# Pooled attention and two feed-forward layers: the SBUF tiles laid out from multiples of 2048 bytes

## The chip, the cores and the metric

The kernel runs on one core of a Trainium2 chip. The metric is device time in microseconds (us), taken as the median of the runs. The engines are TensorE (PE, with its weight loads shown apart as PEld), VectorE (DVE), ScalarE (ACT), GpSimd (POOL) and SyncE (SP, which here only issues DMAs). SBUF, the memory that the engines read and write, has 128 partitions; a place in it is a byte address within a partition, the same in all 128.

## The reference

Two batches of 12,288 tokens with 128 channels. Keys and values are one pooled and projected map of 768 positions; attention is followed by two feed-forward layers, both 128 to 2048 to 128.

```python
kv_pool = kv.reshape(B, H//4, 4, W//4, 4, C).mean(axis=(2, 4))
k = v = kv_pool.reshape(B, -1, C) @ w_sr            # 768 x 128 a batch
s = scale * (q @ k.T)
a = softmax(s)
x = (a @ v).reshape(B*S, D)                         # 24576 x 128
h = x @ w_in;   x = (h * sigmoid(1.702 * h)) @ w_out
h = relu(x @ w2_in);   out = (h * h) @ w2_out
```

Everything is float32, and the kernel keeps nearly that precision with three products of rounded halves, as told below.

## The kernel before

**Tiling.** Everything is kept transposed, channels on the partitions. The tokens come in 48 blocks of 512 (24 a batch). For each block the kernel does the attention and then the two layers. A layer has 16 slices of 128 hidden units: for each, a product into `h_ps` (weights stationary, `x` moving), an activation on ACT into `g_sb`, a split on DVE and ACT into a high and a low half (`ghl`), and a product into `y_ps` (weights stationary, `ghl` moving).

**Three products for one.** A float32 operand is held as two tiles in the fp32r format, high and low (`mm3`, lines 252 to 256): high by high (line 254), high by low (255) and low by high (256). So each product is a trio of matmuls, each with its own load of 128x128 weights and a moving operand of 512 columns (2048 bytes of a partition), or 384 (1536 bytes) for the scores. The first operand of `mm3` is stationary, the second moves. Who reads what:

- `h_ps`: stationary the weights `w1ih`, `w1il` or `W` (second layer), moving `x` (`x1` in the first layer, `x2` in the second);
- `y_ps`: stationary `w1oh`, `w1ol` or `W`, moving `ghl`;
- `s_ps` (scores): stationary `qq`, moving the keys, `kv0` for batch 0 and `KV` for batch 1;
- `av_ps` (attention times values): stationary the values, in `kv0` for batch 0 and in `KV` for batch 1, moving `ahl`.

The trace writes `kv` for the tile `kv0`; the batch-1 tile appears as `KV`. Blocks 0 and 1 do attention with plain float32 operands, and the first two layer passes do the second product so (line 687).

**Order.** The program has no loops on the chip. Every operation is put on record with a cost and a due time (`Plan.op`), `Plan.order` then simulates the engines with these costs and the number of buffers of each ring (`RINGS`, line 259), and the instructions are emitted in that order. TensorE gets the work of several blocks interleaved; `y_ps` of a slice comes `LAG` = 7 slices after its `h_ps`. A tile's address plays no part in this order.

**Where tiles lie.** A pool (`tc.tile_pool`) is a stretch of SBUF; pools follow one another in the order in which they are opened, and inside a pool tiles follow one another in the order of their first use, each padded to 32 bytes. The pool `cp` holds tiles that live through the kernel (line 281 on), `sp` the rings. The first 16,512 bytes of a partition are taken ahead of `cp` (16 KiB of scratch for DMA descriptors, four small constants). From the tile sizes the start addresses are, as remainders:

| tile (in order) | bytes of a partition | start, mod 2048 | start, mod 128 |
|---|---|---|---|
| `ident`, `wsr`, `pooled`, `kf`, `vf` | 512, 512, 3072, 3072, 3072 | 128, 640, 1152, 128, 1152 | 0 |
| `kv0` (keys and values of batch 0) | 12288 | 128 | 0 |
| `minus`; `w1ih`, `w1il`, `w1oh`, `w1ol` | 512; 8192 each | 128; 640 | 0 |
| `qraw` (2), `ghl` (4), second layer's weights (4), `ahl` (2), `y_sb` (2) | 2048, 8192, 8192, 8192, 2048 | 640 | 0 |
| `st` (3) | 48, padded to 64 | 640, 704, 768 | 0, 64, 0 |
| `p_sb`/`pT_sb` (2), `KV` (batch 1), `qq`, `x1` (2), `x2`, `g_sb` (2), `kvraw` (2) | 12288, 12288, 4096, 4096, 4096, 4096, 2048 | 832 | 64 |

The three `st` tiles take 192 bytes, so all that follows them is shifted by 64 against a grid of 128 bytes. Inside a tile the steps are multiples of 512 bytes (weight slices) or 1536 (halves of the keys), so the remainder mod 128 holds for every operand read from it.

Of the kernel before, what the change touches and what calls it, by code (L numbers as in the profile page):

```python
# [10 lines left out]
F32 = mybir.dt.float32  # L11
F32R = mybir.dt.float32r
# [189 lines left out]
def kernel(  # L202
# [20 lines left out]
    P = 128  # L223
    C, NTOK = qT.shape
    B, _, NK, R = kvT.shape
    DFF = w1i.shape[1]
    TB = 512
    NB = NTOK // TB
    NBB = NB // B
    KT = NK // P  # L230
# [10 lines left out]

    cp = ctx.enter_context(tc.tile_pool(name="cp", bufs=1))
    sp = ctx.enter_context(tc.tile_pool(name="sp", bufs=1))
    pp = ctx.enter_context(tc.tile_pool(name="pp", bufs=1, space=bass.MemoryType.PSUM))
    dp = ctx.enter_context(tc.tile_pool(name="dp", bufs=2, space=bass.MemoryType.DRAM))
    c = COST
# [5 lines left out]
    def mm3(out, a, b, start, stop):  # L252
# [9 lines left out]
        pp=(2, [P, QT * NK], F32, sp), aa=(2, [P, 2, 2 * TB], F32R, sp),  # L262
        q=(2, [P, TB], F32, sp), qq=(1, [P, 2, TB], F32R, sp),
        xx=(2, [P, 2, TB], F32R, sp), x2=(1, [P, 2, TB], F32R, sp),
        yo=(2, [P, TB], F32, sp), st=(3, [P, 12], F32, sp), kv=(2, [P, TB], F32, sp), b1=(1, [P, 4, NK], F32R, sp),
        **{f"w{nm}{x}": (1, [P, 2, 2 * TB], F32R, sp) for nm in ("2i", "2o") for x in "hl"},
    )
    plan = Plan({tag: r[0] for tag, r in RINGS.items()})
# [9 lines left out]
        return T[key]  # L278


    ident = cp.tile([P, P], F32, name="ident")
    wsr = cp.tile([P, C], F32, name="wsr")
    pooled = cp.tile([P, NK], F32, name="pooled")
    kf = cp.tile([P, NK], F32, name="kf")
    vf = cp.tile([P, KT, C], F32, name="vf")
    T["KV", 0] = cp.tile([P, 4, NK], F32R, name="kv0")
    minus = cp.tile([P, P], F32R, name="minus")
    for nm in ("1i", "1o"):
        for x in "hl":
            T["W", nm, x] = cp.tile([P, DFF], F32R, name=f"w{nm}{x}")  # L290
# [528 lines left out]
```

## Time and profile before

| | |
|---|---|
| median of 3 runs | 2607.78 us (2607.28 to 2608.26) |
| profiled execution | 2606.7 us, its span 2604.9 us |
| granted TensorE clock, mean | 0.998 of 2.4 GHz |
| PE busy | 2572.7 us (99%), 11260 matmuls |
| PEld busy | 2098.4 us (81%) |
| DVE busy | 2195.5 us (84%) |
| ACT busy | 1853.7 us (71%) |
| POOL busy | 91.7 us (4%) |

The profiled execution has its own time, and it is taken up to the end of the run; the span goes from its first instruction to its last. Matmuls overlap: the trace gives one an end that is modelled, some 0.39 us after its start for 512 columns, while the next begins after about 0.23 us. What a matmul costs the engine when it is never idle is therefore read from the distance of starts in the timeline; the durations are of use for comparing groups with one another. Starts are shown to 0.01 us, so over a run of n matmuls the mean distance is good to about 10 ns / n.

### The profile page before, as it was taken

The page shows a single profiled execution, that of the slowest core. Times are in us where ns is not written, and L with a number is a line of the kernel's source. Part 1 is how long each engine was busy: PE and PEld are TensorE (multiplying, and loading weights), DVE is VectorE, ACT ScalarE, POOL GpSimd, SP SyncE. Part 2 cuts the span into 40 slices and gives each one's busy share as a digit, 9 for nine tenths or more (in the row PEclk, how much of TensorE's full clock was granted, in tenths as well). Part 3 has the DMA queues.
Part 4 walks back from the last instruction along what each step waited for, and adds up shares of the span by engine and source line. Part 5 has one row for each costly group of instructions (what it writes and reads, how often), then busy time and mean ns, then how long its engine had stood idle before and what let it go on. Part 6 is the DMA issues. An engine that isn't in the chain of part 4 may idle for free.

```text
span 2604.9 us, 29500 instructions
## 1 busy us (share of the span) xinstructions
PE 2572.7 (99%) x11260; PEld 2098.4 (81%) x11260; DVE 2195.5 (84%) x2762; ACT 1853.7 (71%) x2117; POOL 91.7 (4%) x98
## 2 busy tenths in 40 slices
PE   6999999999999999999999999999999999999999
PEld 3678888888888888888888888888888888888887
DVE  7898888888888888888888888888888888888876
ACT  4777767776777677776777677767777677767766
POOL 0000000000000000000000000000000000000000
PEclk9999999999999999999999999999999999999999
DMA  4422332223222422223222322232223222232110
GB/s 175 126 61 61 103 84 61 65 89 93 65 61 73 107 68 61 65 86 84 57 57 81 89 57 57 65 101 62 57 57 95 75 57 57 81 89 57 53 53 13
DMA packets 57790, 192.81 MB, mean 74 GB/s; under 512 B 6064, under 2 KB 10288, under 8 KB 51760
## 3 DMA queue, kind: packets, MB, share of 16 engines
q1 hardware_dynamic: 50736, 178.34, 24.5%
q10 hardware_dynamic: 6912, 12.59, 1.5%
q8 instruction: 88, 1.44, 0.2%
q14 instruction: 54, 0.44, 0.1%
HBM read 105.97 MB, written 84.93 MB: 73 GB/s over the span
## 4 chain that ended last, share of the span: by engine, by line
PE 98%; DVE 1%; DMA 1%; ACT 0%; issue 0%; SPq 0%
PE h_ps L255 14%; PE h_ps L254 14%; PE h_ps L256 14%; PE y_ps L255 13%; PE y_ps L256 13%; PE y_ps L254 13%; PE s_ps L256 2%; PE av_ps L254 2%; PE av_ps L255 2%; PE s_ps L255 2%; PE s_ps L254 2%; PE av_ps L256 2%; PE y_ps L687 1%; DMA kvraw<-in_kvT_dram 1%; PE av_ps L610 0%; PE s_ps L498 0%
## 5 line engine op out<-in xcount | busy, mean ns | idle before, releaser
L678 DVE TENSOR_TENSOR ghl<-g_sb,ghl 128x1024 fp32r<-128x1024 f32 x752 | 917.3, 1225 | 74.6 <-ACT ghl L675 53.6
L664 ACT ACTIVATE g_sb<-h_ps 128x1024 f32<-128x1024 f32 x368 | 378.1, 1028 | 393.8 <-PE h_ps L256 278.1
L677 DVE CAST ghl<-g_sb 128x1024 fp32r<-128x1024 f32 x612 | 460.3, 752 | 202.3 <-ACT g_sb L664 153.9
L667 ACT ACTIVATE g_sb<-h_ps 128x1024 f32<-128x1024 f32 x384 | 394.3, 1027 | 129.5 <-PE h_ps L256 118.8
L670 ACT ACTIVATE g_sb<-g_sb 128x1024 f32<-128x1024 f32 x384 | 407.2, 1060 | 6.5
L254 PE MATMUL h_ps<-x,w1ih 128*128 128x512 f32 x768 | 308.5, 402 | 0.2 <-ACT ghl L664 0.2
L254 PE MATMUL h_ps<-x,W 128*128 128x512 f32 x768 | 306.8, 400 | 0.0
L255 PE MATMUL y_ps<-ghl,W 128*128 128x512 f32 x768 | 303.3, 395 | 1.5 <-DVE st L540 1.2
L255 PE MATMUL h_ps<-x,W 128*128 128x512 f32 x768 | 304.2, 396 | 0.0
L255 PE MATMUL h_ps<-x,w1ih 128*128 128x512 f32 x768 | 303.9, 396 | 0.0
L256 PE MATMUL h_ps<-x,W 128*128 128x512 f32 x768 | 303.1, 395 | 0.0
L256 PE MATMUL h_ps<-x,w1il 128*128 128x512 f32 x768 | 302.7, 394 | 0.0
L256 PE MATMUL y_ps<-ghl,W 128*128 128x512 f32 x768 | 301.1, 392 | 0.0
L254 PE MATMUL y_ps<-ghl,W 128*128 128x512 f32 x768 | 300.6, 391 | 0.3 <-DVE ghl L677 0.3
L255 PE MATMUL y_ps<-ghl,w1oh 128*128 128x512 f32 x736 | 289.5, 393 | 0.0
L256 PE MATMUL y_ps<-ghl,w1ol 128*128 128x512 f32 x736 | 289.1, 393 | 0.0
L254 PE MATMUL y_ps<-ghl,w1oh 128*128 128x512 f32 x736 | 287.1, 390 | 0.0
L603 DVE TENSOR_TENSOR ahl<-pT_sb,ahl 128x1024 fp32r<-128x1024 f32 x138 | 164.7, 1221 | 36.4 <-ACT ahl L602 36.4
L511 DVE TENSOR_REDUCE st<-s_ps 128x1 f32<-128x768 f32 x192 | 182.8, 952 | 11.8 <-PE s_ps L256 3.2
L569 DVE STREAM_TRANSPOSE t_sb<-p_sb 128x768 f32<-128x768 f32 x184 | 179.4, 975 | 3.3
L515 ACT ACTIVATE p_sb<-s_ps,st 128x768 f32<-128x768 f32 x192 | 172.9, 901 | 3.3 <-DVE st L511 2.7
L255 PEld LDWEIGHTS y_ps<-ghl,W 128*128 128x128 f32 x768 | 144.3, 188 | 36.9 <-DVE ghl L678 2.9
(104 smaller groups left out, 3797.1 us busy)
## 6 DMA issues: line engine op xcount, KB each, us to landing
way<-t_sb SPq DMA_DIRECT2D x46, 1536.0 KB, 5.1
pT_sb<-way SPq DMA_DIRECT2D x184, 384.0 KB, 7.0
qraw<-in_qT_dram SPq DMA_DIRECT2D x48, 256.0 KB, 9.2
out_dram<-y_sb ACTq DMA_DIRECT2D x48, 256.0 KB, 4.7
kvraw<-in_kvT_dram SPq DMA_DIRECT2D x12, 512.0 KB, 8.8
kvraw<-in_kvT_dram SPq DMA_DIRECT2D x24, 256.0 KB, 7.8
wraw<-in_w1i_dram SPq DMA_DIRECT2D x4, 512.0 KB, 10.3
wraw<-in_w1o_dram SPq DMA_DIRECT2D x4, 512.0 KB, 10.4
```

What stands on the lines that cost most here:

```text
L254: nc.tensor.matmul(out, ah, bh, start=start, stop=False)
L255: nc.tensor.matmul(out, ah, bl, start=False, stop=False)
L256: nc.tensor.matmul(out, al, bh, start=False, stop=stop)
L511: lambda both=both, col=col: nc.vector.tensor_reduce(out=col(0), in_=both(), axis=AX.XY, op=ALU.max, negate=True),
L515: lambda both=both, col=col, p=p: nc.scalar.activation(p().rearrange("p (k a q i) -> p a q k i", k=KT, a=2, q=2) if f32 else p().rearrange ...
L569: plan.op("DVE", c["trans"], at, lambda t=t, p=p: nc.vector.transpose(get(tt)[:, :, t, :], p().rearrange("p (b j) -> p b j", j=32)), reads ...
L603: plan.op("DVE", c["sub1k"], at, lambda ah=ah, al=al, src=src: nc.vector.tensor_sub(four(al()), src(), four(v32(ah()))), reads=[*parts, h] ...
L664: "ACT", c["ev2"], at, lambda G=G, flat=flat: nc.scalar.activation(G(), flat(), AF.Gelu_apprx_sigmoid),
L667: plan.op("ACT", c["ev2"], at, lambda G=G, flat=flat: nc.scalar.activation(G(), flat(), AF.Relu), reads=[(h, 0), (h, 1)], writes=[g])
L670: plan.op("ACT", c["act1k"], at + 0.3, lambda G=G: nc.scalar.activation(G(), G(), AF.Square), writes=[g])
L677: plan.op("DVE", c["cast1k"], at + 0.5, lambda G=G, GH=GH: nc.vector.tensor_copy(GH(), G()), reads=[g], writes=[gh])
L678: plan.op("DVE", c["sub1k"], at + 0.7, lambda G=G, GH=GH, GL=GL: nc.vector.tensor_sub(GL(), G(), v32(GH())), reads=[g, gh], writes=[gl])
```

## The change

A third pool, `ep`, is opened behind `sp`. `pooled`, `kf`, `vf` and the three `st` tiles move there. A tile named `gap` of 384 bytes, which nothing reads or writes, goes ahead of `ident`, and `minus` goes ahead of `kv0`.

```diff
+    ep = ctx.enter_context(tc.tile_pool(name="ep", bufs=1))
...
-        ... st=(3, [P, 12], F32, sp), ...
+        ... st=(3, [P, 12], F32, ep), ...
...
+    cp.tile([P, 96], F32, name="gap")
     ident = cp.tile([P, P], F32, name="ident")
     wsr = cp.tile([P, C], F32, name="wsr")
-    pooled = cp.tile([P, NK], F32, name="pooled")
-    kf = cp.tile([P, NK], F32, name="kf")
-    vf = cp.tile([P, KT, C], F32, name="vf")
+    minus = cp.tile([P, P], F32R, name="minus")
     T["KV", 0] = cp.tile([P, 4, NK], F32R, name="kv0")
-    minus = cp.tile([P, P], F32R, name="minus")
+    pooled = ep.tile([P, NK], F32, name="pooled")
+    kf = ep.tile([P, NK], F32, name="kf")
+    vf = ep.tile([P, KT, C], F32, name="vf")
```

By the sizes, `kv0` now starts at 16,512 + 384 + 3 x 512 = 18,432 = 9 x 2048, and as every later tile of `cp` and `sp` has a multiple of 2048 bytes, all of them start at a multiple of 2048: the weights of both layers, `qraw`, `ghl`, `ahl`, `KV`, `qq`, `x1`, `x2`, and with them `g_sb`, `p_sb`, `pT_sb` and `y_sb`. `pooled` and `vf` start at multiples of 2048 behind them, `kf` and the three `st` tiles follow there. The number of instructions, their order, and what each computes stay as they are.

## Rows read from the trace of the kernel before

**Rows 1.** The page: span, TensorE's busy time, the chain that ended last by engine.
```profile
span 2604.9 us, 29500 instructions
PE 2572.7 (99%) x11260; PEld 2098.4 (81%) x11260; DVE 2195.5 (84%) x2762; ACT 1853.7 (71%) x2117; POOL 91.7 (4%) x98
...
PE 98%; DVE 1%; DMA 1%; ACT 0%; issue 0%; SPq 0%
```

**Rows 2.** Busy us (and instructions) by engine in two stretches, granted clock, DMA share.
```profile
0.00:65.00 65.00, 39.72 (x120) 22.62 (x120) 50.86 (x84) 27.77 (x48) 2.57 (x8) 0.92 0.47 175
...
400.00:600.00 200.00, 200.00 (x888) 165.18 (x887) 172.49 (x215) 142.28 (x160) 8.00 (x8) 1.00 0.30 81
```

**Rows 3.** Waits: who waited for whom, us in total, times, longest.
```profile
PE k_ps L404 <- DMA kvraw<-in_kvT_dram: 13.8, 1, 13.8
...
ACT g_sb L664 <- PE h_ps L256: 278.1, 238, 2.8
```

**Rows 4.** Groups of TensorE by line and tile: count, busy us, mean ns.
```profile
L256 PE MATMUL h_ps<-x,W 128*128 128x512 f32 x768 | 303.1, 395 | 0.0
...
L256 PE MATMUL y_ps<-ghl,W 128*128 128x512 f32 x768 | 301.1, 392 | 0.0
...
L256 PE MATMUL y_ps<-ghl,w1ol 128*128 128x512 f32 x736 | 289.1, 393 | 0.0
...
L256 PE MATMUL s_ps<-KV,qq 128*128 128x384 f32 x192 | 65.1, 339 | 0.0
...
L256 PE MATMUL s_ps<-kv,qq 128*128 128x384 f32 x176 | 59.3, 337 | 0.0
...
L256 PE MATMUL av_ps<-ahl,KV 128*128 128x512 f32 x144 | 56.8, 395 | 0.0
...
L256 PE MATMUL av_ps<-ahl,kv 128*128 128x512 f32 x132 | 51.5, 390 | 0.0
```

**Rows 5.** Timeline of TensorE, a trio of each layer product: start us, us.
```profile
1000.54 0.40 PE L254 MATMUL h_ps<-x,w1ih 128*128 128x512 f32 x1
...
1001.24 0.39 PE L254 MATMUL y_ps<-ghl,W 128*128 128x512 f32 x1
...
1001.93 0.40 PE L254 MATMUL h_ps<-x,w1ih 128*128 128x512 f32 x1
```

**Rows 6.** Timeline of TensorE where batch 0 multiplies by its values.
```profile
973.12 0.39 PE L254 MATMUL av_ps<-ahl,kv 128*128 128x512 f32 x1
...
974.50 0.39 PE L254 MATMUL av_ps<-ahl,kv 128*128 128x512 f32 x1
...
975.85 0.34 PE L254 MATMUL s_ps<-kv,qq 128*128 128x384 f32 x1
...
977.59 0.40 PE L254 MATMUL av_ps<-ahl,kv 128*128 128x512 f32 x1
...
978.98 0.40 PE L254 MATMUL h_ps<-x,W 128*128 128x512 f32 x1
```

**Rows 7.** The same in batch 1.
```profile
1979.51 0.40 PE L254 MATMUL av_ps<-ahl,KV 128*128 128x512 f32 x1
...
1982.31 0.34 PE L254 MATMUL s_ps<-KV,qq 128*128 128x384 f32 x1
...
1983.36 0.39 PE L254 MATMUL y_ps<-ghl,w1oh 128*128 128x512 f32 x1
...
1984.04 0.39 PE L254 MATMUL av_ps<-ahl,KV 128*128 128x512 f32 x1
...
1985.41 0.40 PE L254 MATMUL h_ps<-x,W 128*128 128x512 f32 x1
```

More of the change, by code (lines that the diff above doesn't have):

```diff
@@ L264 @@
         xx=(2, [P, 2, TB], F32R, sp), x2=(1, [P, 2, TB], F32R, sp),
-        yo=(2, [P, TB], F32, sp), st=(3, [P, 12], F32, sp), kv=(2, [P, TB], F32, sp), b1=(1, [P, 4, NK], F32R, sp),
+        yo=(2, [P, TB], F32, sp), st=(3, [P, 12], F32, ep), kv=(2, [P, TB], F32, sp), b1=(1, [P, 4, NK], F32R, sp),
         **{f"w{nm}{x}": (1, [P, 2, 2 * TB], F32R, sp) for nm in ("2i", "2o") for x in "hl"},
```

## The prediction

> **What bounds the kernel now.** I read four views, in this order. First the page's busy times and the chain that ended last: TensorE is busy for 2572.7 of the 2604.9 us of the span and carries 98% of the chain [rows 1]. So the time is what TensorE's instructions cost, laid end to end. Then the stretches: in the first 65 us TensorE works for 39.72 us only, at a granted clock of 0.92; in a steady stretch of 200 us it is busy for all 200.00 us at 1.00, while DVE is busy for 172.49 and ACT for 142.28 us [rows 2]. Third the waits: the longest in which TensorE waits for anybody is 13.8 us, once, for the first keys; in the steady part the waits run the other way, ACT waiting for `h_ps` 238 times, 278.1 us in total [rows 3]. No engine holds TensorE up, and none would until it became some 14% faster (200.00 to 172.49).
>
> So the one question is what a matmul costs, and whether its operands' places have a part in it. That is the fourth view, the timeline: the distance from one start to the next where TensorE is never idle. The granted clock of 1.00 is the level of 2.4 GHz, at which 512 columns take 512 / 2.4 = 213.3 ns. What is seen is more:
>
> - a trio of `h_ps`: 1001.24 - 1000.54 = 0.70 us, 233.3 ns a matmul [rows 5];
> - a trio of `y_ps`: 1001.93 - 1001.24 = 0.69 us, 230.0 ns [rows 5]. Three starts shown to 0.01 us would not separate the two by themselves, but the mean durations of the whole run stand apart the same way, 395 ns for `h_ps` against 392 and 393 for `y_ps` [rows 4];
> - `av_ps` in batch 0: 12 matmuls in 975.85 - 973.12 = 2.73 us and 6 in 978.98 - 977.59 = 1.39 us, so 4.12 us / 18 = 228.9 ns [rows 6];
> - `av_ps` in batch 1: 2.80 us for 12 and 1.37 us for 6, so 4.17 / 18 = 231.7 ns [rows 7].
>
> **The experiment that the kernel before contains.** The last two lines are the same instruction, the same moving tile `ahl`, the same neighbours; what differs is where the stationary values lie: `kv0` starts at a multiple of 128 bytes, `KV` 64 past one (the layout table). The price is 2.8 ns a matmul, and the durations of all of them say so too, 395 against 390 ns [rows 4]. The scores repeat it with the moving operand: 339 ns on `KV`, 337 on `kv0` [rows 4]. And `x1` and `x2`, which move in `h_ps`, lie 64 past such a multiple, while `ghl`, which moves in `y_ps`, lies on one. All three pairs point one way: an operand that starts 64 bytes off a grid of 128 costs TensorE 2 to 3 ns a matmul, whether it is stationary or moving. After the change no operand is off that grid.
>
> **The change part by part.**
>
> The shift of `x1` and `x2` onto the grid: 4608 matmuls of `h_ps` (six groups like the row of 768). The nearest row for a matmul with both operands on the grid is `av_ps` of batch 0 at 228.9 ns, because there, unlike in `y_ps`, no neighbour inside the run is off it. From 233.3 this is 4.4 ns, 20.3 us. The bounds: to the level of `y_ps`, 230.0 ns (15.2 us), and to the lowest level of any trio, 226.7 ns (30.4 us), which is the `y_ps` between 1983.36 and 1984.04: 0.68 us / 3 [rows 7]; the last six of batch 0's first run are as low, 975.85 - 974.50 = 1.35 us / 6 = 225.0 ns, good to 2 ns [rows 6].
>
> `y_ps`, 4512 matmuls (three groups of 768, three of 736): both operands are on the grid of 128 already. They change in what the trace can't show: they now start at multiples of 2048 instead of 128 past a multiple of 512, and their neighbours `h_ps` move onto the grid. I take the level of `av_ps` of batch 0 here too, 1.1 ns, 5.0 us; bounds 0 and, at 226.7 ns, 14.9 us. Below nothing see the second rival.
>
> `KV` of batch 1: 432 matmuls of `av_ps` (three groups of 144) by 2.8 ns, 1.2 us (at 226.7 ns 2.2 us, and 0.9 us for the 396 of batch 0). 576 of `s_ps` (three of 192) by 2 ns, 1.2 us. `qq`, stationary in all 1104 matmuls of `s_ps`, goes onto the grid too: between nothing and the 2.8 ns of `av_ps`, half of it taken, 1.5 us (ends 0 and 3.1).
>
> `pooled`, `kf`, `vf`, `minus`, `ident` and `wsr` are read in the first blocks only, where TensorE waits for keys anyway [rows 2, 3]: nothing. `st`, a few columns for DVE and ACT, nothing. `gap` is never touched. `g_sb`, `p_sb`, `pT_sb` and `y_sb` move for DVE, ACT and the DMAs; should these become slower or faster by some per cent, the cover is the 27.5 us in 200 that DVE is not busy [rows 2]. No wait, DMA or instruction is added or moved.
>
> The sum: 20.3 + 5.0 + 1.2 + 1.2 + 1.5 = 29.2 us. The profiled execution took 2606.7 us, 1.1 below the median of 2607.8; the forecast for the median is 2607.8 - 29.2 = 2578.6 us.
>
> **The rivals.**
>
> Only the grid of 128 counts, and each matmul's level is its own. Then `h_ps` falls to 230.0 ns, `KV` to the level of `kv0`, and the rest stays: 15.2 + 1.2 + 1.2 = 17.6 us, 2590.2 us. For it: `y_ps` is at 230.0 with both operands on the grid. Against it: the same `y_ps` at 226.7 ns in another neighbourhood [rows 7].
>
> The other side: multiples of 2048 are no better than 64 past the grid, and 128 past a multiple of 512 was the good place (all the cheaper rows lie there, and none at a multiple of 256). Then `h_ps` and `KV` stay, and what was cheap rises to their level: `y_ps` to 233.3 ns (3.3 x 4512 = 14.9 us), `av_ps` of batch 0 by 2.8 ns x 396 = 1.1 us, its scores by 2 x 528 = 1.1 us, in all 17.1 us: 2624.9 us. It decides as soon as `y_ps` rises by more than `h_ps` falls. Against it: nothing in the rows says that a rounder address is worse.
>
> Everything on the grid goes to the lowest level, 226.7 ns: 30.4 + 14.9 + 2.2 + 0.9 + 1.2 + 3.1 = 52.7 us, 2555.1 us. For it: that level exists with just such operands [rows 6, 7]. Against it: only in short runs.
>
> All that is over the columns' time is address cost and goes: 213.3 ns, so 20.0 x 4608 + 16.7 x 4512 + 18.4 x 432 + 15.6 x 396 ns = 181.6 us, 2426 us. Against it: no trio is below 226 ns by more than its rounding. The Trainium skill, "TensorE: Matmul & The Clock Gate", section "Back-to-back issue gap", gives N / 2.4 + 2.5 ns for a warm matmul; by that estimate this case would end 9948 x 2.5 ns = 25 us later than with 213.3 ns, and no run of this case shows such a gap.
>
> The layout counts for nothing, and the differences come from the product and its neighbours: 2607.8 us. For it: a `y_ps` trio takes 0.69 us at one place and 0.68 at another, with operands at the same remainders [rows 5, 7]. Against it: rows 6 and 7, equal but for the place. The Trainium skill, "SBUF — State Buffer", sections "Specifications (TRN2)" and "Who interferes with whom", speaks for this rival: its lines are of 16 bytes, all tiles start at whole ones before and after, and TensorE is said never to wait on anyone. By that rule the change is worth 0 us; the trace differs, with 231.7 against 228.9 ns.
>
> **How the numbers follow.** The forecast (2566 to 2584) has 0.36, the grid of 128 alone (2584 to 2602) 0.26, the lowest level (2548 to 2566) 0.14, all address cost gone 0.05, no effect 0.11, slower 0.08. No change means within 0.2% (5.2 us), about what a measurement of this kernel can tell. So faster 0.36 + 0.26 + 0.14 + 0.05 = 0.81, same 0.11, slower 0.08. The range takes in the first three, 0.76, and, drawn to 2604, the edge of no effect: 2548 to 2604.
>
> **What would show it.** In the timeline after, a trio of `h_ps` takes as long as one of `y_ps`, 0.68 to 0.69 us, and 18 `av_ps` of batch 1 as long as 18 of batch 0. The groups' mean durations show no gap between `KV` and `kv`. A steady 200 us holds some 10 matmuls more than 888. TensorE keeps 98% of the chain and DVE's share of the span rises to 85%. I am wrong if `h_ps` keeps 0.70 us with `x` at its new place (the product sets it), if `y_ps` rises (the good place was lost), or if TensorE's idle time grows in the steady part (another engine pays).

## The result, and the profile after

The changed kernel takes 2569.39 us (median of 4 runs, 2568.68 to 2570.12) against 2608.02 us before: a ratio of 0.9852 (95% interval 0.9835 to 0.9869), 38.6 us less. That is 9 us faster than the forecast of 2578.6 us and inside the range (2548 to 2604).

The page of the changed kernel, lines as in [rows 1]:

```profile
span 2566.9 us, 29500 instructions
PE 2534.8 (99%) x11260; PEld 2100.4 (82%) x11260; DVE 2191.0 (85%) x2762; ACT 1852.8 (72%) x2117; POOL 94.5 (4%) x98
...
PE 98%; DVE 1%; DMA 1%; ACT 1%; issue 0%; SPq 0%
```

The span is 38.0 us shorter and TensorE's busy time 37.9 us; the other engines work as long as before. So the whole gain lies in what TensorE's instructions cost. The steady stretch of 200 us (columns as in [rows 2]) says the same:

```profile
400.00:600.00 200.00, 200.00 (x900) 167.75 (x899) 173.56 (x216) 144.68 (x164) 8.19 (x8) 1.00 0.29 81
```

900 matmuls instead of 888, at the same granted clock of 1.00, and TensorE still never idle. ACT goes on waiting for `h_ps`, no less than before [rows 3]:

```profile
ACT g_sb L667 <- PE h_ps L257: 295.7, 227, 2.8
```

The groups of TensorE, as in [rows 4]. In this program the three products of `mm3` stand one line further down, at 255 to 257 (257 is what 256 was), and ACT's line 664 at 667; in the experiments that open a fourth pool `mm3` stands at 256 to 258.

```profile
L257 PE MATMUL h_ps<-x,W 128*128 128x512 f32 x768 | 300.1, 391 | 0.0
L257 PE MATMUL y_ps<-ghl,W 128*128 128x512 f32 x768 | 299.5, 390 | 0.0
...
L257 PE MATMUL y_ps<-ghl,w1ol 128*128 128x512 f32 x736 | 287.8, 391 | 0.0
L257 PE MATMUL s_ps<-KV,qq 128*128 128x384 f32 x192 | 65.5, 341 | 0.0
L257 PE MATMUL s_ps<-kv,qq 128*128 128x384 f32 x176 | 60.0, 341 | 0.0
L257 PE MATMUL av_ps<-ahl,KV 128*128 128x512 f32 x144 | 56.3, 391 | 0.0
L257 PE MATMUL av_ps<-ahl,kv 128*128 128x512 f32 x132 | 51.7, 391 | 0.0
```

These groups of 512 columns (the third product of each trio) now stand at 390 to 391 ns, where the same groups stood between 390 and 395: the difference between `h_ps` and `y_ps` is gone, and the one between `KV` and `kv` too. The scores went the other way, from 337 and 339 to 341 ns.

The timeline of TensorE after, starts first: a trio of `h_ps` and one of `y_ps` [rows 5], the values and scores of batch 0 [rows 6] and of batch 1 [rows 7]:

```profile
961.66 0.39 PE L255 MATMUL av_ps<-ahl,kv 128*128 128x512 f32 x1
...
964.38 0.33 PE L255 MATMUL s_ps<-kv,qq 128*128 128x384 f32 x1
...
965.45 0.39 PE L255 MATMUL y_ps<-ghl,w1oh 128*128 128x512 f32 x1
...
966.15 0.39 PE L255 MATMUL av_ps<-ahl,kv 128*128 128x512 f32 x1
...
967.53 0.39 PE L255 MATMUL h_ps<-x,W 128*128 128x512 f32 x1
...
988.78 0.39 PE L255 MATMUL h_ps<-x,w1ih 128*128 128x512 f32 x1
...
989.46 0.39 PE L255 MATMUL y_ps<-ghl,W 128*128 128x512 f32 x1
...
990.14 0.39 PE L255 MATMUL h_ps<-x,w1ih 128*128 128x512 f32 x1
...
1952.19 0.39 PE L255 MATMUL av_ps<-ahl,KV 128*128 128x512 f32 x1
...
1954.91 0.33 PE L255 MATMUL s_ps<-KV,qq 128*128 128x384 f32 x1
```

Both layer trios take 0.68 us, 226.7 ns a matmul, and 12 matmuls with values take 2.72 us in either batch, 226.7 ns as well (before 2.73 and 2.80 us). That is the level which the prediction called the lowest. Six scores take 965.45 - 964.38 = 1.07 us, and the `y_ps` behind them 0.70 us. Before, these are 1.05 us, from 975.85 [rows 6] to the start of the `y_ps` behind them, and 0.69 us:

```profile
976.90 0.40 PE L254 MATMUL y_ps<-ghl,w1oh 128*128 128x512 f32 x1
...
977.59 0.40 PE L254 MATMUL av_ps<-ahl,kv 128*128 128x512 f32 x1
```

Where the 38 us are, by the mean distance from a matmul's start to the next (worked out from the starts in the two traces; distances of 0.3 us and more, 38 in each trace and nearly all in the first 165 us, are left out): `h_ps` 233.2 to 227.4 ns, 5.8 x 4608 = 26.7 us; `y_ps` 230.2 to 227.4, 2.8 x 4512 = 12.6 us; `av_ps` of batch 1 232.0 to 227.9, 4.1 x 432 = 1.8 us, of batch 0 228.9 to 228.0, 0.9 x 396 = 0.4 us; scores of batch 0 174.2 to 177.9, 3.7 x 528 = 2.0 us lost, of batch 1 176.5 to 177.6, 1.1 x 576 = 0.6 us lost. The sum is 38.9 us.

### The profile page after: what moved, and what is told of

Same layout as the page of the kernel before. It is cut to its first block, busy times and chain, and to the rows that moved or that the text cites. A ratio compares the mean times of both kernels' runs of the same rounds, so it can differ in the third digit from the quotient of the medians.

```text
span 2566.9 us, 29500 instructions
## 1 busy us (share of the span) xinstructions
PE 2534.8 (99%) x11260; PEld 2100.4 (82%) x11260; DVE 2191.0 (85%) x2762; ACT 1852.8 (72%) x2117; POOL 94.5 (4%) x98
## 4 chain that ended last, share of the span: by engine, by line
PE 98%; DVE 1%; DMA 1%; ACT 1%; issue 0%; SPq 0%
PE h_ps L256 14%; PE h_ps L257 13%; PE h_ps L255 13%; PE y_ps L256 13%; PE y_ps L257 13%; PE y_ps L255 13%; PE s_ps L257 3%; PE s_ps L255 3%; PE s_ps L256 2%; PE av_ps L257 2%; PE av_ps L256 2%; PE av_ps L255 2%; PE y_ps L690 1%; DMA kvraw<-in_kvT_dram 1%; PE av_ps L613 0%; PE s_ps L501 0%
## 5 line engine op out<-in xcount | busy, mean ns | idle before, releaser
L255 PE MATMUL h_ps<-x,w1ih 128*128 128x512 f32 x768 | 303.9, 396 | 0.2 <-ACT ghl L667 0.2
L255 PE MATMUL h_ps<-x,W 128*128 128x512 f32 x768 | 302.3, 394 | 0.0
L256 PE MATMUL h_ps<-x,W 128*128 128x512 f32 x768 | 300.3, 391 | 0.0
L257 PE MATMUL h_ps<-x,W 128*128 128x512 f32 x768 | 300.1, 391 | 0.0
L256 PE MATMUL h_ps<-x,w1ih 128*128 128x512 f32 x768 | 299.3, 390 | 0.0
L255 PEld LDWEIGHTS h_ps<-x,w1ih 128*128 128x128 f32 x768 | 144.3, 188 | 33.3 <-issue 1.9
```

Of the source, the lines that this page charges most:

```text
L255: nc.tensor.matmul(out, ah, bh, start=start, stop=False)
L256: nc.tensor.matmul(out, ah, bl, start=False, stop=False)
L257: nc.tensor.matmul(out, al, bh, start=False, stop=stop)
```

## The experiments

All stand on the kernel before or after and only move tiles; the program's order is the same in all. Beside the time, one more number is read from each trace: the distance between two fixed instructions, the first `av_ps` matmul of a block of batch 0 (973.12 us before, 961.66 us after) and of a block of batch 1 (1979.51 and 1952.19 us), with 4456 matmuls from the one to the other and TensorE never idle. It is 1006.39 us before and 990.53 us after. Four traces whose layouts should be alike (after, and experiments 1, 2 and 9) agree in it to 0.01 us, so it shows differences that the times can't. The kernel before was timed again beside each experiment; its medians lie between 2606.9 and 2607.9 us, so differences to after, which was timed once, are good to about 1 us.

**1. The `st` tiles alone** (against before):

```diff
+    ep = ctx.enter_context(tc.tile_pool(name="ep", bufs=1))
-        ... st=(3, [P, 12], F32, sp), ...
+        ... st=(3, [P, 12], F32, ep), ...
```

> The kernel before, with the three st tiles alone moved behind sp. Everything that TensorE reads in the steady part then starts at a multiple of 128 bytes, but 128 or 640 past a multiple of 2048. Grid theory (only an offset of 64 against a grid of 128 costs, for each operand by itself): as after, 2569 us, trios of h_ps and y_ps both at 0.68 us. Rounder-address theory (multiples of 256 or more are what brought y_ps down): y_ps stays at 0.69 us, h_ps falls to it, 15 to 18 us faster than before, 2590 us. Relative theory (the offset between the weights being loaded and the operand that moves counts, not the address itself): as after, 2569 us.

Measured: 2569.14 us, ratio to before 0.9854 (0.9837 to 0.9870).

```profile
962.36 0.39 PE L255 MATMUL av_ps<-ahl,kv 128*128 128x512 f32 x1
...
989.48 0.39 PE L255 MATMUL h_ps<-x,w1ih 128*128 128x512 f32 x1
...
990.16 0.39 PE L255 MATMUL y_ps<-ghl,W 128*128 128x512 f32 x1
...
990.84 0.39 PE L255 MATMUL h_ps<-x,w1ih 128*128 128x512 f32 x1
...
1952.89 0.39 PE L255 MATMUL av_ps<-ahl,KV 128*128 128x512 f32 x1
```

990.53 us between the two, to the last digit what after has. So the 192 bytes of `st` are the whole change: `gap`, the new place of `minus`, and the multiples of 2048 give nothing. The rounder-address theory falls; the grid and the relative theory forecast the same and are not parted. The run shows one thing more. `ghl` and the weights lie ahead of `st`, so `y_ps` reads from the very addresses that it read from before. Yet its trio takes 0.68 us (990.16 to 990.84), and over all its trios it falls from 230.2 to 227.4 ns, as in after. So all that `y_ps` lost before it lost to what its neighbours read.

**2. Everything shifted by 64 bytes** (against after):

```diff
-    cp.tile([P, 96], F32, name="gap")
+    cp.tile([P, 112], F32, name="gap")
```

> The kernel after with a gap 64 bytes longer: every tile of cp and sp starts 64 past a multiple of 2048, so all operands are off the grid of 128 but unchanged against one another. Grid theory: both operands of every matmul are off, each worth about 3 ns: h_ps and y_ps at 0.70 us a trio or more, 2608 us or slower. Relative theory: no change against after, 2569 us, trios at 0.68 us.

Measured: 2568.26 us (2567.75 to 2569.79).

```profile
962.77 0.39 PE L255 MATMUL av_ps<-ahl,kv 128*128 128x512 f32 x1
...
1953.30 0.39 PE L255 MATMUL av_ps<-ahl,KV 128*128 128x512 f32 x1
```

990.53 us again, although nothing that TensorE reads in the layers, the scores and the values lies on a grid of 128 bytes any more. This is the run that brings down the reading on which the prediction rested: a shift that all operands share costs nothing. What counts is how the places stand to one another.

**3. `x1` and `x2` alone off by 64** (against after; experiments 6, 7 and 9 differ only in the size of `off`: 32, 8 and 64 words for 16):

```diff
+    xp = ctx.enter_context(tc.tile_pool(name="xp", bufs=1))
...
+    xp.tile([P, 16], F32, name="off")
...
-        xx=(2, [P, 2, TB], F32R, sp), x2=(1, [P, 2, TB], F32R, sp),
+        xx=(2, [P, 2, TB], F32R, xp), x2=(1, [P, 2, TB], F32R, xp),
```

> The kernel after with x1 and x2 alone 64 past a multiple of 2048 (moving operand of h_ps; its weights stay on the grid). Both grid and relative theory: h_ps goes from 0.68 to 0.70 us a trio, about 5.8 ns a matmul x 4608 = 27 us slower than after, 2596 us, y_ps unchanged at 227.4 ns. Neighbour theory (a matmul is slowed by the one before it): y_ps rises to 230 ns as well, 2609 us.

Measured: 2612.98 us, 43.6 more than after and slower than before (1.0022, 1.0013 to 1.0031).

```profile
976.04 0.40 PE L256 MATMUL av_ps<-ahl,kv 128*128 128x512 f32 x1
...
1003.61 0.40 PE L256 MATMUL h_ps<-x,w1ih 128*128 128x512 f32 x1
...
1004.30 0.40 PE L256 MATMUL y_ps<-ghl,W 128*128 128x512 f32 x1
...
1005.00 0.40 PE L256 MATMUL h_ps<-x,w1ih 128*128 128x512 f32 x1
...
1984.61 0.40 PE L256 MATMUL av_ps<-ahl,KV 128*128 128x512 f32 x1
```

1008.57 us. Not only the trio of `h_ps` has gone up (0.69 us); the trio of `y_ps`, whose operands did not move, takes 0.70 us. Over all trios the two stand at 232.2 and 232.1 ns. So of the three theories the neighbour theory holds, with a price 4 us above its 2609: a matmul pays for its neighbours' operands too. With experiment 1 that is why `y_ps` was at 230 ns before, with both its operands in step, and the reason that the prediction took too little for it. The price is not the same as before, where `x` stood 64 bytes on the other side of its weights (64 against 128): there `h_ps` had 233.2 and `y_ps` 230.2 ns. So the direction may count here too, though before has `qq` and `KV` off as well; `x` at 192 was not run.

**4. `qq` alone off by 64** (against after; 8, 11 and 12 with 8, 32 and 48 words):

```diff
+    xp = ctx.enter_context(tc.tile_pool(name="xp", bufs=1))
...
+    xp.tile([P, 16], F32, name="off")
...
-        q=..., qq=(1, [P, 2, TB], F32R, sp),
+        q=..., qq=(1, [P, 2, TB], F32R, xp),
```

> The kernel after with qq alone 64 past a multiple of 2048 (stationary operand of s_ps; the keys that move stay on the grid). Grid theory: the scores become slower by up to 3 ns x 1104 = 3 us, 2572 us. Relative theory, with the sign seen in before (scores of batch 0 with just these offsets took 174.2 ns, those of after take 178.0 and 177.6): the scores become faster by 3.5 ns x 1104 = 4 us, 2565 us.

Measured: 2564.83 us (2564.37 to 2565.45), 4.6 less than after.

```profile
962.55 0.34 PE L256 MATMUL s_ps<-kv,qq 128*128 128x384 f32 x1
...
963.60 0.40 PE L256 MATMUL y_ps<-ghl,w1oh 128*128 128x512 f32 x1
```

1.05 us for six scores: the 1.05 us of before, where `qq` and `kv0` stood 64 apart too, in the other direction (experiment 12 repeats that direction). For the matmuls of 384 columns being in step is the worse place. The sign of the relative theory held; the grid theory had it wrong.

**5. The weights of both layers alone off by 64** (against after; the pool `xp` and an `off` of 16 words as in experiment 3):

```diff
-            T["W", nm, x] = cp.tile([P, DFF], F32R, name=f"w{nm}{x}")
+            T["W", nm, x] = xp.tile([P, DFF], F32R, name=f"w{nm}{x}")
...
-        **{f"w{nm}{x}": (1, [P, 2, 2 * TB], F32R, sp) ...
+        **{f"w{nm}{x}": (1, [P, 2, 2 * TB], F32R, xp) ...
```

> The kernel after with the weights of both layers alone 64 past a multiple of 2048: stationary in h_ps and y_ps; x and ghl, which move, stay on the grid, so no two matmuls in a row differ in where their moving operand lies. Weight theory (the offset between the weights that are being loaded and the operand that moves meanwhile): h_ps and y_ps both go to 231 to 233 ns, 9120 matmuls by some 5 ns = 45 us slower than after, 2614 us. Moving theory (what costs is that one matmul's moving operand lies otherwise than the one before): nothing changes, 2569 us.

Measured: 2623.21 us, ratio to before 1.0061 (1.0046 to 1.0076), 54 more than after.

```profile
979.93 0.40 PE L256 MATMUL av_ps<-ahl,kv 128*128 128x512 f32 x1
...
1007.56 0.39 PE L256 MATMUL h_ps<-x,w1ih 128*128 128x512 f32 x1
...
1008.26 0.40 PE L256 MATMUL y_ps<-ghl,W 128*128 128x512 f32 x1
...
1008.96 0.39 PE L256 MATMUL h_ps<-x,w1ih 128*128 128x512 f32 x1
...
1992.42 0.40 PE L256 MATMUL av_ps<-ahl,KV 128*128 128x512 f32 x1
```

0.70 us for either trio, 1012.49 us for the stretch. Inside the layers the moving operands are all in step with one another, and so are the loads; only loads and moving operands stand apart. So the offset between what a load reads and what moves costs by itself. In the steady part nobody else uses these tiles: the trace of before has their last write at 161.5 us, and from then on TensorE alone reads them. So the price isn't one of another engine's access to them. The Trainium skill, "TensorE: Matmul & The Clock Gate", section "Step-by-step: what each phase is for", has the load and the moving operand on two independent read ports. If that meant that neither takes anything from the other, this run would take as long as after; it takes 54 us more.

**6, 7 and 9. How far off is off.** `x1` and `x2` alone at 128, at 32 and at 256 bytes.

> The kernel after with x1 and x2 alone 128 past a multiple of 2048. If the period of the offset is 128 bytes: as after, 2569 us, trios at 0.68 us. If it is 256 or more: h_ps and y_ps rise as they did with x at 64, 2590 to 2613 us.

> The kernel after with x1 and x2 alone 32 past a multiple of 2048. If only whole steps of 64 bytes count: as after, 2569 us. If the price grows with the offset: between after and the 2613 us of x at 64, say 2590 us.

> The kernel after with x1 and x2 alone 256 past a multiple of 2048. If the offset between the weights and the moving operand counts modulo 256: as after, 2569 us. If modulo 512 (the length of one row of a weight slice): h_ps and y_ps rise to 231 to 232 ns as they did at 32, 64 and 128, about 2609 us.

Measured: 2608.84 us at 128, 2608.55 us at 32, 2569.05 us at 256. At 128 and at 256:

```profile
976.76 0.39 PE L256 MATMUL av_ps<-ahl,kv 128*128 128x512 f32 x1
...
1983.41 0.39 PE L256 MATMUL av_ps<-ahl,KV 128*128 128x512 f32 x1
```

```profile
961.84 0.39 PE L256 MATMUL av_ps<-ahl,kv 128*128 128x512 f32 x1
...
1952.38 0.39 PE L256 MATMUL av_ps<-ahl,KV 128*128 128x512 f32 x1
```

1006.65 and 990.54 us (at 32: 1006.57). An offset of 32 costs as much as one of 128, some 39 us against 44 at 64, so the price doesn't grow with the offset; and 256 costs nothing: for `x` the offset acts modulo 256. (256 is also the control for the move to `xp`: the other pool alone costs nothing.) The grid of 128 was half of that; before had only offsets of 64 (64 against 128, modulo 256), which can't tell the two apart.

**8, 11 and 12. `qq` at 32, 128 and 192.**

> The kernel after with qq alone 32 past a multiple of 2048. With qq at 64 the scores took 175.3 ns instead of 177.8 and the time was 4.5 us less. If only whole steps of 64 bytes count: as after, 2569 us. If 32 does as 64 does or better: 2565 us or less.

> The kernel after with qq alone 128 past a multiple of 2048. At 0 the scores took 177.8 ns, at 32 and 64 some 175 ns, and the time was 3.3 and 4.5 us less than after. If the offset acts modulo 256 or more, 128 again differs from 0: scores at 175 ns or less, 2565 us. If it does nothing: 2569 us.

> The kernel after with qq alone 192 past a multiple of 2048. Times so far: 2569.4 us at 0, 2566.0 at 32, 2564.8 at 64, 2563.2 at 128. If only the distance from a multiple of 256 counts, whichever side: 192 is as 64, 2564.8 us. If the direction counts (the load starting earlier or later in its 256 bytes than the keys): another value, between 2561 and 2569 us, and if it is below 2563 the best version so far.

Measured: 2566.03, 2563.22 (2562.11 to 2564.62) and 2563.86 us (2563.47 to 2564.45); the stretch 989.53, 988.50 and 988.51 us, with `qq` at 64 989.00 us. At 128:

```profile
962.12 0.34 PE L256 MATMUL s_ps<-kv,qq 128*128 128x384 f32 x1
...
963.19 0.40 PE L256 MATMUL y_ps<-ghl,w1oh 128*128 128x512 f32 x1
...
963.88 0.39 PE L256 MATMUL av_ps<-ahl,kv 128*128 128x512 f32 x1
...
965.24 0.39 PE L256 MATMUL h_ps<-x,W 128*128 128x512 f32 x1
```

Over all scores the mean is 175.2 ns (batch 0) and 174.7 ns (batch 1) at 32, but 177.6 and 177.4 ns at 128. The rows at 128 show it: six scores take 1.07 us, as in after; what is shorter comes behind them: 0.69 us for the `y_ps` trio and 1.36 us for the six `av_ps`, in after 0.70 and 967.53 - 966.15 = 1.38 us. So the expectation that the scores themselves would fall to 175 ns missed at 128, and the time was gained in the matmuls of 512 columns: over all of them `h_ps`, `y_ps` and `av_ps` stand at 227.0 ns, in after at 227.4 to 228.0. The starts show where the difference lies (165 groups of scores, from 300 us on). In after the three trios behind a group of scores take 232.8, 230.3 and 230.6 ns a matmul, and 226.7 from the fourth on; with `qq` at 128 the first takes 230.0 and the next ones 226.6 to 226.7. At 32 the scores are faster, but the time lies between the two expectations. At 192 the scores gain and what follows them does not:

```profile
962.67 0.34 PE L256 MATMUL s_ps<-kv,qq 128*128 128x384 f32 x1
...
963.71 0.40 PE L256 MATMUL y_ps<-ghl,w1oh 128*128 128x512 f32 x1
...
964.41 0.40 PE L256 MATMUL av_ps<-ahl,kv 128*128 128x512 f32 x1
...
965.79 0.39 PE L256 MATMUL h_ps<-x,W 128*128 128x512 f32 x1
```

Six scores take 1.04 us (174.4 and 174.0 ns over all of batch 0 and of batch 1), while the trio and the six behind them keep 0.70 and 1.38 us. 192 is 64 on the other side, the place that `qq` had against `kv0` before, and the scores of batch 0 had 174.2 ns there. It is not as 64 (the stretch is 0.49 us shorter, and the scores had 175.1 ns there in batch 1), so the direction counts. The times at 128 and 192 can't be told apart, though the gain lies in other matmuls; no place tried gives both. Both beat the kernel before (0.9830, 0.9815 to 0.9844, at 128) and the changed one, by some 6 us.

**10. `x1`, `x2` and their own weights off by 64 together** (against after): `xp`, with an `off` of 16 words, for `xx`, `x2`, `w1ih`, `w1il` and the second layer's `w2i`; the rest stays.

> The kernel after with x1, x2 and the weights that meet them (w1ih, w1il and the second layer's w2i) all 64 past a multiple of 2048; ghl and its weights stay. Inside a trio the offset of weights to moving operand is nothing again; it is 64 only where a trio of h_ps follows one of y_ps or the other way, in one load of three. Pair theory (the offset between the load and the operand that moves meanwhile): one matmul in three pays what all paid with the weights off (14 cycles more than after, 5.8 ns): 9120 / 3 x 5.8 ns = 18 us, about 2587 us. Moving theory (a change of place from one moving operand to the next): as with x alone at 64, 2613 us. If only offsets inside a trio counted: 2569 us.

Measured: 2605.46 us, ratio to before 0.9993 (0.9984 to 1.0002), 36 more than after.

```profile
974.50 0.40 PE L256 MATMUL av_ps<-ahl,kv 128*128 128x512 f32 x1
...
1980.24 0.40 PE L256 MATMUL av_ps<-ahl,KV 128*128 128x512 f32 x1
```

1005.74 us. None of the three theories gave this number. Inside a trio everything is in step, yet 36 of the 44 us of experiment 3 are paid. Where trios of `h_ps` and `y_ps` alternate, and if a load runs while the matmul before it moves its operand (the trace starts both together), the loads out of step with what moves meanwhile are 2 in 6 here, 3 in 6 with `x` alone off, 6 in 6 with the weights off; the prices, 36, 44 and 54 us, grow far less than these counts. So a step out seems to cost more than the one matmul in which it happens; experiment 11 shows that for the step from the scores.

## Why the prediction was right, and where not

**The bound.** Right: TensorE, laid end to end, nothing else [rows 1 to 3]; no new wait came, and the cover of DVE held (173.56 us in 200).

**The reading of the experiment inside the kernel before.** The observation was right and its rule wrong. `av_ps` on `KV` and on `kv` differ by their place [rows 6, 7], and so does `h_ps`. But "64 past a grid of 128 costs, each operand by itself" fails three times: with all operands there the time is that of after (experiment 2), `x` at 128, on the grid, costs 39 us, nearly what 64 does (experiments 6 and 3), and `y_ps` falls without its operands having moved (experiment 1). What the runs support is: the operands that TensorE reads for matmuls of 512 columns in a row, moving and stationary, should start alike modulo 256 bytes (256 itself was run for `x` alone). Before, `ghl`, `ahl`, `kv0` and the weights were at 128 modulo 256 and `x1`, `x2`, `KV`, `qq` at 64, moved there by 192 bytes of `st`; after, all are at 0. Both rules call the layout after the good one, and so the forecast had the right sign and most of the size (29.2 of 38.6 us). In that it was lucky: the change put right a condition that the prediction didn't know, and the layout of experiment 6, in which all operands lie on the grid of 128 too, takes 2608.84 us, no less than before.

**`h_ps`**, forecast 4.4 ns and 20.3 us: measured 5.8 ns and 26.7 us, inside its bounds (15.2 to 30.4).

**`y_ps`**, forecast 1.1 ns and 5.0 us: measured 2.8 ns and 12.6 us. This term was the worst sized of the gains. Both its operands were taken to be in their good place already, and it was to gain a little from its neighbours; experiment 1 shows that all it lost came from them, and experiment 3 that with `x` put off again it pays as much as `h_ps`. The lone `y_ps` trio of 0.68 us [rows 7] was the hint.

**`KV` with the values**, forecast 1.2 us: measured 1.8 us, and 0.4 us in batch 0, which was set at nothing.

**The scores**, forecast 1.2 us for `KV` and 1.5 us for `qq`, both gains: measured 2.6 us lost. The rule was carried from 512 columns to 384, where it has the other sign (experiments 4 and 8). The prediction read the 339 ns on `KV` against 337 on `kv0` [rows 4] as a third pair that pointed its way. It was the warning: `qq` was in step with `KV` and out of step with `kv0`, and the scores out of step were the faster ones.

**The rivals.** "Only the grid of 128 counts" (2590.2 us) fell with `y_ps` at 227.4 ns. "The lowest level everywhere" (2555.1 us) is 14 us too fast, further off than the forecast, but its terms for the layers (30.4 and 14.9 us) are nearer to the measured 26.7 and 12.6 than the forecast's: the trios of the layers stand at 226.7 ns except in the three trios behind the scores, and what lacks is the scores and what follows them. No effect (2607.8 us) and slower (2624.9 us) fell. The Trainium skill, "SBUF — State Buffer", sections "Specifications (TRN2)" and "Who interferes with whom", has lines of 16 bytes and a TensorE that never waits on anyone, by which the layout would be worth nothing; the trace differs, as 32 bytes, two such lines, cost 39 us in experiment 7. "All address cost gone" (2426 us) fell too: where trios of a layer follow one another, no run has them below 226.7 ns for long.

**What stays open.** Why modulo 256, why 384 columns want another offset than 512, why the direction counts, and by what rule the prices of single steps out of line add up. Behind the scores one is paid for nine matmuls in after and for three or fewer with `qq` at 128; in the layers, where the next step comes sooner, the distances of starts fit no price for a single event. A layout with the weights at other offsets than 64, `x` at 192, and keys moved instead of `qq` were not tried, and neither was any other type of operand than fp32r.

## What to carry to other kernels

Where TensorE is the bound and never idle, read the distance of starts group by group; groups of the same shape that differ by 2 to 6 ns may be telling of where their tiles lie, and a tile of a few bytes in the middle of a pool is enough to shift all that follow it. Put small tiles last and let what TensorE reads in a row start alike modulo 256 bytes, as was best here for fp32r with a load for each matmul of 512 columns; a shift of everything together did not matter. Then try other offsets for matmuls of another length, one tile at a time: here 128 bytes on `qq` gave another 6 us.

## What the runs showed of the hardware that was not expected

- A trio of 128x512 matmuls in the fp32r format, each with its own weight load, takes 680 ns at best, at a granted clock of 1.00 (2.4 GHz): 226.7 ns a matmul. With the weights 64 bytes off the moving operand it takes 700 ns, 233.3 ns a matmul.
- The place of the weights alone moves the kernel from 2569 to 2623 us, with TensorE busy for 99% of the span and 98% of the chain in both; these shares don't show it, only the distances of starts and the busy time itself do (2534.8 and 2590.0 us).
- Tiles that start at 0, at 64 (experiment 2), or at 128 and 640 past a multiple of 2048 (experiment 1) leave a stretch of 4456 matmuls at 990.53 us to the last digit, while `x` 32 bytes off the rest makes it 1006.57 us.
- A matmul can lose 2.8 ns to its neighbours' places alone: `y_ps`, its own operands at unchanged addresses, went from 230.2 to 227.4 ns when its neighbours' moved (experiment 1).
